# DeltaNet plus mixture of experts on one core: where the zero fills are issued, which engine scales v, and the shape of the old state's products

## Chip, cores, metric

One Trainium2 chip, one of its cores. The metric is device time in microseconds of one execution; the profile of one execution shows what its engines did. TensorE is PE (its weight loads PEld), VectorE DVE, ScalarE ACT, GpSimd POOL, SyncE SP. SP, ACT and POOL also issue DMAs; an engine executes and issues its instructions in the order in which they are written.

## The reference, cut

```python
# attention: 4 batches, 8 heads, 768 steps, head dimension 48
k_n = k / (norm(k) + 1e-6); state = 0
for t in range(S):
    y[t]  = q[t] @ state                       # output from the old state
    v_old = k_n[t] @ state
    state = state + beta[t] * outer(k_n[t], v[t] - v_old)
# then, on the 3072 rows of y (8 heads x 48 = 384 wide):
logits = x @ w_gate; e = argmax(logits); gate = softmax(logits)[e]
out = gate * (relu(x @ w1[e]) @ w2[e])         # 8 experts, 384 -> 1024 -> 384
```

## The kernel before

The 768 steps are cut into 6 blocks of 128 for each of the 4 batches: 24 tiles n = 4*tb + b. Inside a tile the recurrence is solved in four pieces of 32 steps. The main loop is a software pipeline of 27 ticks t; in tick t piece q of tile t - q is worked on, so four tiles are in flight.

The recurrence needs, for each block tb, 32 inverses of 32x32 triangular systems. `prepare(tb)` makes the scales (square roots, reciprocals) from `lg`, the products of the keys within each piece, and multiplies `lg` by row scales (line 323, 128x1024); `lanes(tb)` then does 31 column steps of multiply and subtract on DVE (lines 353 and 360) and one transpose (366) into `wt`. For block 0 `lg` comes from PE directly; for blocks 1 to 5 the products in `gg` go to DRAM `gd` (line 248) and come back as `lg` (line 251) in another layout. Each tile's `kpart` (transposes, line 217; copy to `kt`, 221; products, 259; copy to `gg`, 244) must have run first.

A tick: `residual` (PE, lines 392 and 404, and DVE line 411, which subtracts from v); `apply` (PE 419 multiplies with `wt`, ACT 423 copies to `u`); `scale_v` of the next tick (line 375, v times the norms in `nt`); `finish` of the tile three ticks back: the old state's output `yp` (line 435), the state's update (444, 448), the rest of the output (453), then the routing of its rows. `emit_slots` does the routing's small DVE steps for two tiles at a time and scatters their rows by indirect DMA (line 550, on POOL) into `xg`, a DRAM table with 448 slots for each expert, or `xt`. `xg` and `xt` are zeroed first (line 766): 7 fills of 512 rows, one of 64 and 8 of 64.

Between these, `beside(t, i)` is called seven times a tick: it runs `STEPS[i]` steps of the inverses, three steps of the routing (four from tick 20), and other pieces. The order of each engine's work is the order of the calls; nothing reorders it. Before the loop, `INIT` and `FILL` are hand-written orders of the first tiles' parts; then 56 steps of `lanes(0)`, `prepare(1)`, the rest of `lanes(0)`.

[...] After the loop the experts' products run on PE (lines 650, 660, 940); the first expert's start is fitted into the last ticks.

Of the kernel before, what the change touches and what calls it, by code (L numbers as in the profile page):

```python
# [13 lines left out]
ALU = mybir.AluOpType  # L14
# [4 lines left out]
B, H, S, D = 4, 8, 768, 48  # L19
# [21 lines left out]
def deltanet_moe(ctx, tc, q, k, v, beta, w_gate, w1, w2, out):  # L41
    nc = tc.nc
# [22 lines left out]
    zrow = cp.tile([128, ROW], F32, name="zrow")  # L65
# [41 lines left out]
    INIT = (0, 1, -2, 2, 0, 'l', 1, 'l', 'l', 3, 2, 'l', 'l', 'l', 'l', -1, 3, 'l', -1, 'l', 'l', 'l', 'l', 'l',  # L107
            -4, -1, 'l')

    STEPS = (3, 3, 2, 3, 2, 2, 2)  # L110
    W1 = 4
    DM2 = 0
    DEF = 2
# [35 lines left out]
    nt_t = lp.tile([128, (NT * B + LAG) * H], F32, name="nt_all")  # L149
# [135 lines left out]
    def prepare(tb):  # L285

        T = tiles[tb]
        if tb == 0:
            T["lg"] = fp.tile([128, 32, 32], F32, name="lg0", tag="lg", bufs=2)
        lg = T["lg"]  # L290
        lw = T["lw"]
        ss, s0, r0 = (lp.tile([128, 32], F32, name=f"{n_}{tb}", tag=n_) for n_ in ("ss", "s0", "r0"))
        if tb == 0:
            nc.vector.transpose(out=ss, in_=sst)
            yield
            nc.vector.tensor_scalar(out=ss, in0=ss, scalar1=1e-36, scalar2=None, op0=ALU.max)
        else:
            nc.vector.tensor_scalar(out=ss, in0=lg.rearrange("p a b -> p (a b)")[:, 0:1024:33],
                                    scalar1=1e-36, scalar2=None, op0=ALU.max)
        for _ in range(6 if tb > 1 else 1):  # L300
            yield
        nc.scalar.activation(out=s0, in_=ss, func=AF.Sqrt)
        yield
        nc.vector.reciprocal(r0, s0)
        yield
        nc.vector.tensor_tensor(out=r0, in0=r0, in1=ss, op=ALU.mult)
        yield
        nc.vector.tensor_tensor(out=s0, in0=s0, in1=r0, op=ALU.add)
        yield
        nc.vector.tensor_scalar(out=s0, in0=s0, scalar1=0.5, scalar2=1e-6, op0=ALU.mult, op1=ALU.add)  # L310
        yield
        nc.vector.reciprocal(r0, s0)
        yield
        nc.vector.tensor_tensor(out=ss, in0=r0, in1=bl[:, tb, :], op=ALU.mult)
        yield
        nc.vector.tensor_tensor(out=lw.rearrange("p a b -> p (a b)")[:, 0:1024:33], in0=ss, in1=r0, op=ALU.mult)
        yield
        nc.vector.tensor_tensor(out=r0, in0=ss, in1=r0, op=ALU.mult)
        yield
        if tb == 0:  # L320
            nc.vector.transpose(out=lg, in_=tiles["dg"].rearrange("p h t -> p t h"))
            yield
        nc.gpsimd.tensor_tensor(out=lg, in0=lg, in1=r0.unsqueeze(2).broadcast_to([128, 32, 32]), op=ALU.mult)  # L323
        for q in range(NB):
            p = slice(32 * q, 32 * q + 32)
            nc.vector.transpose(out=nt_t[p, (B * tb + q) * H:(B * tb + q) * H + 32], in_=s0[p])
            yield
        T["nt"] = True
# [42 lines left out]
    def scale_v(t):  # L371

        vn = vt[t]
        for r in rows(t):
            nc.gpsimd.tensor_tensor(out=vn[r], in0=vn[r], in1=nt_t[r, t * H:(t + 1) * H].unsqueeze(2)
                                    .broadcast_to([r.stop - r.start, H, D]), op=ALU.mult)

    def clear_u(n):
# [4 lines left out]
    def uview(n):  # L383
        return us[n].rearrange("t (h d) -> t h d", h=H)
# [42 lines left out]
    def finish(n):  # L427

        tb, b = n // B, n % B
        last = tb == NT - 1  # L430
        st, u = st_t[b], uview(n)
        qt, pm = qt_t[n % QSL], pm_t[n % QSL]
        yp = pss.tile([128, NP, C], F32, name=f"yp{tb}_{b}", tag="y", bufs=YB)
        for p in range(NP):
            nc.tensor.matmul(yp[:, p, :], lhsT=st[:, p, :], rhs=qt[:, p, :],  # L435
                             start=(p == 0), stop=True, skip_group_check=True)
        yield
        if not last:
            ku = pss.tile([112, NP, D], F32, name=f"ku{tb}_{b}", tag="y", bufs=YB)
            for h in range(H):  # L440

                m = 64 if h % 2 == 0 else D
                kn = tiles[tb][b]["kn"].rearrange("t h d -> t (h d)")[:, h * D:h * D + m]
                nc.tensor.matmul(ku[64 * (h % 2):64 * (h % 2) + m, h // 2, :], lhsT=kn, rhs=u[:, h, :],
                                 start=True, stop=True, skip_group_check=True)
            for a in range(2):
                r = slice(64 * a, 64 * a + D)
                nc.vector.tensor_tensor(out=st[r, :, r], in0=st[r, :, r], in1=ku[r], op=ALU.add)
            if n + NB_ < NN - B:
                load_ku(n + NB_)  # L450
        yield
        for h in range(H):
            nc.tensor.matmul(yp[64 * (h % 2):64 * (h % 2) + D, h // 2, :], lhsT=u[:, h, :], rhs=pm[:, h, :],  # L453
                             start=False, stop=True, skip_group_check=True)
        yt = lp.tile([128, NP, C], F32, name=f"yt{tb}_{b}", tag="yt", bufs=2)
        nc.scalar.copy(out=yt, in_=yp)
        yield
        w = 1 if n >= NN - W1 else 2
        if n % w == 0:
            tiles["row", n // w, w] = (rp if n < NN - 2 else xq_[0]).tile([128, 2 if n < NN - 2 else 1, ROW], F32, name=f"row{tb}_{b}", tag="row", bufs=2)  # L460
            tiles["rl", n // w, w] = lp.tile([128, 2, E], F32, name=f"rl{tb}_{b}", tag="rl", bufs=2)
        row, rl = tiles["row", n // w, w], tiles["rl", n // w, w]
        row, rl = row[:, 0:w], rl[:, 0:w]
        emit_x(n, yt, row[:, n % w], rl[:, n % w])
        if n % w == w - 1:
            fine.append(emit_slots(tb, b - w + 1, w, row, rl))
# [257 lines left out]
    NN = NT * B  # L724
# [12 lines left out]
    for i in range(NB):  # L737
        nc.sync.dma_start(out=bl[32 * i:32 * i + 32],
                            in_=beta.rearrange("b h (t i s) -> i (b h) t s", t=NT, i=NB)[i])
# [22 lines left out]
    slots = [xg[i:i + 512, :].rearrange("(g p) c -> p g c", p=128) for i in range(0, n0, 512)]  # L762
    slots.append(xg[n0:E * CAP + 512 - CAP, :].unsqueeze(1))
    slots += [xt[e * CAP + NG * 128:e * CAP + NG * 128 + 64, :].unsqueeze(1) for e in range(E)]
    for x in slots:
        nc.scalar.dma_start(out=x, in_=zrow[0:x.shape[0]].unsqueeze(1).broadcast_to(x.shape))
    while "nt" not in tiles[0]:
        run(lane)
    scale_v(0)
# [41 lines left out]
    def beside(t, i):  # L811

        inverses(STEPS[i], t)
        if before and (t, i) >= (B * before[0][0] - 5, 3):
            if not run(before[0][1], 3):
                before.pop(0)
        for _ in range(3 if t < NN - B else 4):
            if fine and not run(fine[0]):
                fine.pop(0)
        for _ in range(WSL.count((t, i))):  # L820
            run(W)
        for _ in range(ES.count((t, i))):
            ahead_step()

    fin = iter(())
    for t in range(NN + LAG):
        if t < NN and t % B == 0 and t > 0:
            while queue and queue[0][0] <= t // B:
                inverses(1, t)
            if t == NN - B:  # L830
                ep_.close()
                wq.append(ep.enter_context(tc.tile_pool(name="wr", bufs=1, side="right")))
                xq_.append(ep.enter_context(tc.tile_pool(name="xq", bufs=1, side="right")))
                W = pieces()
                run(W)
        residual(t)
        beside(t, 0)
        chunk(ks_, t)
        chunk(qs_, t)
        run(fin)  # L840
        if t + 1 < NN + LAG:
            scale_v(t + 1)
        if t + 1 < NN:
            clear_u(t + 1)
        beside(t, 1)
        copies = apply(t)
        run(copies)
        for tb in range(1, NT):
            for i in range(NB):
                if t == B * (tb - 1) + i:  # L850
                    load_v(tb, i)
        fin = finish(t - LAG) if t >= LAG else iter(())
        run(fin)
        beside(t, 2)
        run(fin)
        run(copies)
        beside(t, 3)
        chunk(ks_, t)
        beside(t, 4)
        run(fin)  # L860
        beside(t, 5)
        chunk(qs_, t)
        beside(t, 6)
    i = 0
    run(fin)
    while fine:
# [102 lines left out]
    op = ctx.enter_context(tc.tile_pool(name="op", bufs=1))  # L969
# [44 lines left out]
    for n0 in range(B * NT):  # L1014
# [3 lines left out]
                                     in_=idc, in_offset=None)  # L1018
    LP = tc.For_i(0, nblk, 1)
    LP.__enter__()  # L1020
    if True:
        ind, sel, t8 = small("ind"), small("sel"), small("t8")
        ei, j0, ce, r, rc, gi, ov = (small(n_, (128, 1)) for n_ in ("ei", "j0", "ce", "r", "rc", "gi", "ov"))
# [59 lines left out]
        for f in range(KF):  # L1083
            ps = po.tile([128, 128], F32, name="oph")
            for j in range(KD):
                nc.tensor.matmul(ps, lhsT=ow1[:, j, f * 128:(f + 1) * 128], rhs=xt[:, j, :],
                                 start=(j == 0), stop=(j == KD - 1))
            nc.scalar.activation(out=ht[:, f, :], in_=ps, func=AF.Relu)
        ps = po.tile([128, DM], F32, name="opy")
        for f in range(KF):  # L1090
# [4 lines left out]
                                     in_=yo, in_offset=None, bounds_check=N - 1, oob_is_err=False)  # L1095
# [29 lines left out]
```

## Time and profile before

| | us |
|---|---|
| median of 3 runs (604.93 to 608.1) | 607.08 |
| the profiled execution | 609.56 |
| its span, first to last instruction | 607.8 |
| busy in us: PE / DVE / ACT / POOL | 519.2 / 379.0 / 266.2 / 133.3 |

The profiled execution is 2.48 us over the median, and 1.76 us of it lie outside the span. Three stretches have to be read apart: the start up to the first line 411 at 68.1 us, the ticks up to about 355 us, and the experts after that. [...] A row "A <- B" of the waits says that A stood idle until B was done.

### The profile page before, as it was taken

The numbers are of one execution on the slowest core, as the hardware profiler recorded it, in microseconds if no ns is written. First come the engines' busy times: TensorE is split into PE (matmuls) and PEld (weight loads), VectorE is DVE, ScalarE is ACT, GpSimd is POOL, SyncE is SP. The second block draws the span as 40 slices with busy tenths as digits, with TensorE's granted clock in tenths as the row PEclk, the third lists the DMA queues.
The fourth block names the chain that finished last, engine by engine and source line by source line (L and its number), as shares of the span: only waits on it lengthen the run. The fifth ranks groups of instructions, "written<-read, shape, count | busy, mean of one in ns | idle before, by whom it ended". The sixth has DMA issues, their size and how long they took to land. (4 is left out here: it accounts for less than half of the span.)

```text
span 607.8 us, 17613 instructions
## 1 busy us (share of the span) xinstructions
PE 519.2 (85%) x7284; PEld 471.5 (78%) x7285; DVE 379.0 (62%) x1338; ACT 266.2 (44%) x506; POOL 133.3 (22%) x156
## 2 busy tenths in 40 slices
PE   7146478998988897778979989999999999999992
PEld 4035467887877786667868889999999999999992
DVE  5950898898899979994544347636272736455211
ACT  2026155664655554445643326435353625344320
POOL 2600123143333325242322111020201010101111
PEclk9559599998999988998989989999999999999996
DMA  9987348578478556448361245636373646362000
GB/s 200 309 225 129 84 103 183 109 153 207 108 156 204 121 126 147 112 92 241 118 198 56 95 145 165 191 109 200 100 204 111 189 123 184 118 172 76 23 17 24
DMA packets 153636, 85.51 MB, mean 141 GB/s; under 512 B 121565, under 2 KB 147534, under 8 KB 153552
## 3 DMA queue, kind: packets, MB, share of 16 engines
q1 hardware_dynamic: 145680, 68.22, 45.8%
q0 software_dynamic: 3456, 9.57, 4.4%
q10 hardware_dynamic: 4416, 6.56, 3.4%
q8 instruction: 58, 0.95, 0.7%
q14 instruction: 26, 0.21, 0.1%
HBM read 54.05 MB, written 24.37 MB: 129 GB/s over the span
## 5 line engine op out<-in xcount | busy, mean ns | idle before, releaser
L353 DVE TENSOR_TENSOR tmp<-lg,lw 128x84 f32<-128x84 f32 (+26 forms) x372 | 93.0, 290 | 2.0 <-POOL lg L323 1.7
L660 PE MATMUL y<-w2h,hx 128*128 128x384 f32 x352 | 93.4, 339 | 0.0
L360 DVE TENSOR_TENSOR lw<-lw,tmp 128x84 f32<-128x84 f32 (+26 forms) x372 | 85.3, 270 | 0.3
L663 POOL DMA_INDIRECT out_dram<-yo,idx x32 | 30.7, 958 | 225.7 <-ACT yo L935 170.5
L583 DVE TENSOR_TENSOR w2l<-w2r,w2h 128x768 fp32r<-128x768 f32 x32 | 31.2, 977 | 76.2 <-ACT w2h L582 76.2
L423 ACT COPY u<-ks 32x384 f32<-32x384 f32 x96 | 45.1, 470 | 46.1 <-PE ks L419 42.5
L660 PEld LDWEIGHTS y<-w2h,hx 128*128 128x128 f32 x352 | 63.9, 188 | 0.9
L650 PE MATMUL h<-xh,w1h 128*128 128x448 f32 x168 | 61.4, 365 | 0.0
L650 PE MATMUL h<-xh,w1l 128*128 128x448 f32 x168 | 61.3, 365 | 0.0
L650 PE MATMUL h<-xl,w1h 128*128 128x448 f32 x168 | 61.3, 365 | 0.0
L660 PE MATMUL y<-w2l,hx 128*128 128x384 f32 x176 | 59.0, 335 | 0.0
L419 PE MATMUL ks<-v_all,wt 32*32 32x48 f32 x1536 | 25.4, 207 | 35.6 <-DVE v_all L411 35.5
L419 PEld LDWEIGHTS ks<-v_all,wt 32*32 32x32 f32 x1536 | 21.4, 108 | 40.1 <-DVE v_all L411 38.4
L654 DVE SCALAR_TENSOR_TENSOR hx<-h,hx 128x448 fp32r<-128x448 f32 (+1 forms) x64 | 36.9, 587 | 23.7 <-ACT hx L653 23.4
L277 POOL TENSOR_SCALAR_AFFINE_SELECT pm<-pm 128x1024 f32<-128x1024 f32 x24 | 26.9, 1119 | 104.4 <-ACT pm L276 104.3
L653 ACT ACTIVATE hx<-h 128x448 fp32r<-128x448 f32 (+1 forms) x64 | 32.3, 516 | 37.2 <-PE h L650 37.2
L935 ACT ACTIVATE yo<-y,gt 128x384 f32<-128x384 f32 x22 | 12.8, 582 | 74.7 <-PE y L660 60.3
L259 PE MATMUL pg<-kt 64*128 64x128 f32 x384 | 32.4, 313 | 13.2 <-ACT kt L221 11.0
L392 PE MATMUL ks<-st,kt 128*32 128x96 f32 x768 | 43.3, 250 | 0.0
L550 POOL DMA_INDIRECT xg<-row,sli x22 | 27.5, 1251 | 63.5 <-DMA xg<-row,sli 34.0
L259 PEld LDWEIGHTS pg<-kt 64*128 64x128 f32 x384 | 27.5, 214 | 16.4 <-ACT kt L221 11.4
L392 PEld LDWEIGHTS ks<-st,kt 128*32 128x32 f32 x768 | 32.4, 110 | 3.5 <-issue 0.4
(169 smaller groups left out, 1086.2 us busy)
## 6 DMA issues: line engine op xcount, KB each, us to landing
w1r<-in_moe_w_dram SPq DMA_DIRECT2D x24, 512.0 KB, 4.1
w2r<-in_moe_w_dram SPq DMA_DIRECT2D x32, 384.0 KB, 3.4
xg<-zrow ACTq DMA_DIRECT2D x7, 788.0 KB, 7.9
kn<-in_k_dram SPq DMA_DIRECT2D x24, 192.0 KB, 5.0
qn<-in_q_dram SPq DMA_DIRECT2D x24, 192.0 KB, 4.8
xr<-xg SPq DMA_DIRECT2D x7, 591.0 KB
xn<-row SPq DMA_DIRECT2D x10, 394.0 KB
ku<-in_k_dram SPq DMA_DIRECT2D x20, 192.0 KB, 3.1
```

The source lines that it names most:

```text
L259: nc.tensor.matmul(pg[a][:, p], lhsT=kt[r, p], rhs=xt[r, p], start=True, stop=True, tile_position=(64 * a, 0), skip_group_check=True)
L353: nc.vector.tensor_tensor(out=x, in0=lg[:, r0:r1, c:c + 1].broadcast_to([128, r1 - r0, b - a]), in1=lw[:, c:c + 1, a:b].broadcast_to([128, ...
L360: nc.vector.tensor_tensor(out=lw[:, r0:r1, a:b], in0=lw[:, r0:r1, a:b], in1=x, op=ALU.subtract)
L392: nc.tensor.matmul(ks[32 * q:32 * q + 32, 2 * p:2 * p + 2, :], lhsT=kt_t[n % KSL][:, p, 32 * q:32 * q + 32], rhs=st_view(n % B, p), start= ...
L419: nc.tensor.matmul(ks[r, h, :], lhsT=tiles[n // B]["wt"][r, n % B * H + h, :], rhs=vn[r, h, :], start=True, stop=True, tile_position=(32 * ...
L423: nc.scalar.copy(out=uview(n)[r], in_=ks[r])
L583: nc.vector.tensor_tensor(out=lo, in0=src, in1=hi.bitcast(F32), op=ALU.subtract)
L650: nc.tensor.matmul(ps, lhsT=w[:, d, fs], rhs=x_[:, d], start=(n == 0), stop=(n == len(terms) - 1))
L653: nc.scalar.activation(out=hh, in_=ps, func=AF.Relu)
L654: nc.vector.scalar_tensor_tensor(out=hl, in0=ps, scalar=0.0, in1=hh.bitcast(F32), op0=ALU.max, op1=ALU.subtract)
L660: nc.tensor.matmul(ps, lhsT=h(f)[h_], rhs=w2[w][:, f, :], start=(n == 0), stop=(n == len(terms) - 1))
L663: nc.gpsimd.indirect_dma_start(out=out, out_offset=bass.IndirectOffsetOnAxis(ap=idx, axis=0), in_=yo, in_offset=None, bounds_check=N - 1, ...
```

## The change

Four edits. The 16 zero fills of `xg` and `xt` move from ACT's queue ahead of the loop to SP's queue at the end of the ticks: two after tick 0, then one a tick up to tick 14. Both multiplications on POOL, `scale_v` and the row scales of `lg`, move to DVE. The old state's output, four products of 128x128 by 128x128 whose off-diagonal 64x64 blocks are zeros, becomes eight products of 64x64 by 64x128, at the corners (0, 0) and (64, 64) of the array. And one step of the inverses moves from the fourth to the third call of `beside`, and the routing gets as many steps as the inverses there, 17 a tick and not 21, up to tick 19.

```diff
-    STEPS = (3, 3, 2, 3, 2, 2, 2)
+    STEPS = (3, 3, 3, 2, 2, 2, 2)
...
-        nc.gpsimd.tensor_tensor(out=lg, in0=lg, in1=r0.unsqueeze(2).broadcast_to([128, 32, 32]), op=ALU.mult)
+        nc.vector.tensor_tensor(out=lg, in0=lg, in1=r0.unsqueeze(2).broadcast_to([128, 32, 32]), op=ALU.mult)
...
-            nc.gpsimd.tensor_tensor(out=vn[r], in0=vn[r], in1=nt_t[r, t * H:(t + 1) * H].unsqueeze(2)
+            nc.vector.tensor_tensor(out=vn[r], in0=vn[r], in1=nt_t[r, t * H:(t + 1) * H].unsqueeze(2)
...
         for p in range(NP):
-            nc.tensor.matmul(yp[:, p, :], lhsT=st[:, p, :], rhs=qt[:, p, :],
-                             start=(p == 0), stop=True, skip_group_check=True)
+            for a in range(2):
+                r = slice(64 * a, 64 * a + 64)
+                nc.tensor.matmul(yp[r, p, :], lhsT=st[r, p, r], rhs=qt[r, p, :], start=(p == 0), stop=True,
+                                 tile_position=(64 * a, 64 * a), skip_group_check=True)
...
-    for x in slots:
-        nc.scalar.dma_start(out=x, in_=zrow[0:x.shape[0]].unsqueeze(1).broadcast_to(x.shape))
...
-        for _ in range(3 if t < NN - B else 4):
+        for _ in range(STEPS[i] if t < NN - B else 4):
             if fine and not run(fine[0]):
                 fine.pop(0)
...
         chunk(qs_, t)
         beside(t, 6)
+        for x in slots[t + 1 if t else 0:t + 2]:
+            nc.sync.dma_start(out=x, in_=zrow[0:x.shape[0]].unsqueeze(1).broadcast_to(x.shape))
```

ACT's order at the start, before: behind the copy of tile 3's `kt` stand the 16 fills, then the copies of tiles 4 and 5 and of their products.

```order
L302 ACTIVATE s_250<-ss_249 128x32
L221 COPY kt_125<-pt_3_291 128x512
L766 DMA xg<-zrow 128x4x394 x7
L766 DMA xg<-zrow 64x394
L766 DMA xt<-zrow 64x394 x8
L221 COPY kt_126<-pt_0_445 128x512
L221 COPY kt_127<-pt_1_452 128x512
L244 COPY gg_104<-pg_0_0_459 128x4x128
```

The same place now:

```order
L302 ACTIVATE s_250<-ss_249 128x32
L221 COPY kt_125<-pt_3_291 128x512
L221 COPY kt_126<-pt_0_429 128x512
L221 COPY kt_127<-pt_1_436 128x512
L244 COPY gg_104<-pg_0_0_443 128x4x128
```

The fills are gone from between them; nothing else of ACT's order there differs.

DVE's order where block 0's scales end and its column steps begin, before and now. `r_251` holds the row scales, `s_250` the norms, `nt_all` their transpose.

```order
L318 TENSOR_TENSOR r_251<-ss_249,r_251 128x32
L321 STREAM_TRANSPOSE lg_248<-dg 128x1024
L326 STREAM_TRANSPOSE nt_all<-s_250 32x32 x4
L353 TENSOR_TENSOR tmp_0_594<-lg_248,lw_183 128x15
L353 TENSOR_TENSOR tmp_0_594<-lg_248,lw_183 128x16
```

```order
L318 TENSOR_TENSOR r_251<-ss_249,r_251 128x32
L321 STREAM_TRANSPOSE lg_248<-dg 128x1024
L323 TENSOR_TENSOR lg_248<-lg_248,r_251 128x1024
L326 STREAM_TRANSPOSE nt_all<-s_250 32x32 x4
L375 TENSOR_TENSOR v_all<-v_all,nt_all 32x384
L353 TENSOR_TENSOR tmp_0_578<-lg_248,lw_183 128x15
```

Both multiplications now stand on DVE ahead of the column steps; line 375 reads the first load of v.

SP's order around the end of tick 0, now (line 866 is the fills' new place; before, the same rows stood there without it):

```order
L177 DMA qn_120<-in_q_dram 128x8x48
L381 DMA u_784<-zrow 96x384
L201 DMA v_all<-in_v_dram 32x32x48
L866 DMA xg<-zrow 128x4x394 x2
L174 DMA kn_118<-in_k_dram 128x8x48
L177 DMA qn_121<-in_q_dram 128x8x48
L381 DMA u_898<-zrow 96x384
L201 DMA v_all<-in_v_dram 32x24x48
L203 DMA v_all<-in_v_dram 32x8x48
L866 DMA xg<-zrow 128x4x394
```

The loads of the next tick's keys, queries and v stand behind the fills.

## The prediction

> **What bounds the kernel now.** I read the busy time by stretches first (columns: PE, PEld, DVE, ACT and POOL busy, then the granted clock, the share of the DMA engines and GB/s).
>
> ```profile
> 0.00:20.00 20.00, 11.27 (x285) 6.82 (x286) 12.25 (x42) 3.95 (x7) 6.34 (x21) 0.95 0.97 228
> 20.00:40.00 20.00, 3.02 (x14) 2.22 (x16) 18.38 (x104) 1.07 (x2) 6.64 (x17) 0.50 0.95 267
> 40.00:60.00 20.00, 16.22 (x169) 13.36 (x166) 0.19 (x1) 11.32 (x22) 0.82 (x1) 0.86 0.89 160
> 100.00:120.00 20.00, 18.96 (x476) 17.04 (x476) 17.74 (x78) 12.61 (x27) 5.70 (x5) 1.00 0.70 153
> 400.00:500.00 100.00, 100.00 (x540) 94.31 (x539) 47.74 (x76) 42.61 (x70) 12.04 (x13) 1.00 0.50 149
> ```
>
> From 400 us on PE never stops, and no edit touches that. In the ticks DVE and PE are both near full. The start is odd: from 20 to 40 DVE works and PE and ACT stand, from 40 to 60 it is the other way round. Then the waits:
>
> ```profile
> PE ks L419 <- DVE v_all L411: 35.5, 16, 10.2
> ACT kt L221 <- DMA esel<-in_moe_w_gate_dram: 27.8, 1, 27.8
> DVE ss L298 <- DMA lg<-gd: 25.4, 5, 21.4
> ```
>
> and the start in order of time:
>
> ```profile
> 9.80 12.60 SPq L174 DMA_DIRECT2D kn<-in_k_dram  x4
> ...
> 11.01 20.50 ACTq L766 DMA_DIRECT2D xg<-zrow  x7
> 11.36 0.19 DVE L306 TENSOR_TENSOR r<-r,ss 128x32 f32<-128x32 f32 x1
> ...
> 18.88 0.27 DVE L353 TENSOR_TENSOR tmp<-lg,lw 128x15 f32<-128x15 f32 x2 [1.27 <-POOL lg L323]
> ...
> 21.83 1.11 PE L217 MATMUL pt<-ident,kn 128*128 128x128 f32 x4 [6.82 <-DMA kn<-in_k_dram]
> ...
> 38.04 0.34 DVE L360 TENSOR_TENSOR lw<-lw,tmp 128x48 f32<-128x48 f32 x2
> 38.57 1.07 ACT L221 COPY kt<-pt 128x512 f32<-128x512 f32 x2 [27.80 <-DMA esel<-in_moe_w_gate_dram]
> ...
> 40.64 0.82 POOL L375 TENSOR_TENSOR v_all<-v_all,nt_all 32x384 f32<-32x384 f32 x1 [13.53 <-DMA v_all<-in_v_dram]
> ...
> 50.88 2.60 SPq L248 DMA_DIRECT2D gd<-gg  x4
> ```
>
> ```profile
> 59.74 0.19 DVE L298 TENSOR_SCALAR ss<-lg 128x32 f32<-128x32 f32 x1 [21.36 <-DMA lg<-gd]
> ...
> 63.12 2.05 DVE L353 TENSOR_TENSOR tmp<-lg,lw 128x36 f32<-128x36 f32 x2
> ...
> 68.11 0.52 DVE L411 TENSOR_TENSOR v_all<-v_all,ks 32x384 f32<-32x384 f32 x1
> ...
> 71.56 0.41 DVE L353 TENSOR_TENSOR tmp<-lg,lw 128x84 f32<-128x84 f32 x2
> ...
> 72.20 0.42 DVE L353 TENSOR_TENSOR tmp<-lg,lw 128x96 f32<-128x96 f32 x2
> ```
>
> This is the whole case. Tile 4's keys, asked for from 9.80, reach PE at 21.83, since the fills fill the DMA engines (share 0.97). ACT's instruction stream sits in issuing fills until 38.57 (the row's name is the last counter it waited on), though tile 4's transposes lay ready at 22.9. Only then do `kt`, the products, `gd` (50.88) and `lg` (59.74) follow, and DVE, done with its 56 steps at 38.38, stands for 21.36 us. The first tick's line 411 comes at 68.11.
>
> In the ticks DVE is stretched. Its instructions take longer while POOL computes:
>
> ```profile
> 101.72 1.09 POOL L277 TENSOR_SCALAR_AFFINE_SELECT pm<-pm 128x1024 f32<-128x1024 f32 x1 [8.02 <-ACT pm L276]
> 101.73 1.12 DVE L306 TENSOR_TENSOR r<-r,ss 128x32 f32<-128x32 f32 x1
> ...
> 113.16 1.05 DVE L353 TENSOR_TENSOR tmp<-lg,lw 128x96 f32<-128x96 f32 x2
> ...
> 113.24 0.85 POOL L375 TENSOR_TENSOR v_all<-v_all,nt_all 128x384 f32<-128x384 f32 x1
> ```
>
> ```profile
> 133.10 2.52 DVE L353 TENSOR_TENSOR tmp<-lg,lw 128x84 f32<-128x84 f32 x2
> ...
> 133.45 1.11 POOL L277 TENSOR_SCALAR_AFFINE_SELECT pm<-pm 128x1024 f32<-128x1024 f32 x1
> 134.12 0.75 PEld L419 LDWEIGHTS ks<-v_all,wt 32*32 32x32 f32 x64
> 134.12 0.88 PE L419 MATMUL ks<-v_all,wt 32*32 32x48 f32 x64
> ...
> 134.51 0.84 POOL L375 TENSOR_TENSOR v_all<-v_all,nt_all 128x384 f32<-128x384 f32 x1
> 134.93 0.97 PEld L435 LDWEIGHTS yp<-qt,st 128*128 128x128 f32 x8
> 134.93 1.16 PE L435 MATMUL yp<-qt,st 128*128 128x128 f32 x8
> ...
> 136.62 1.16 PE L259 MATMUL pg<-kt 64*128 64x128 f32 x16
> ```
>
> Line 306 takes 0.19 us alone and 1.12 beside the select; the pair of 128x96 takes 0.42 alone and 1.05 beside `scale_v`; the pair of 128x84 takes 0.41 alone and 2.52 where select and `scale_v` come in a row. So POOL's work costs DVE nearly its own length: 0.93 a select, 0.63 to 0.84 a `scale_v`.
>
> **The change part by part. Fills off ACT, the start.** Durations for the sum:
>
> ```profile
> L411 DVE TENSOR_TENSOR v_all<-v_all,ks 128x384 f32<-128x384 f32 (+3 forms) x28 | 15.4, 551 | 10.5 <-issue 4.0 <-POOL pm L277 4.0 <-PE ks L404 2.2
> L323 POOL TENSOR_TENSOR lg<-lg,r 128x1024 f32<-128x1024 f32 x6 | 11.5, 1911 | 44.3 <-DVE r L318 31.5 <-DVE nt_all L326 12.8
> L583 DVE TENSOR_TENSOR w1l<-w1r,w1h 128x1024 fp32r<-128x1024 f32 x24 | 29.5, 1229 | 7.5 <-ACT w1h L582 7.0
> ```
>
> ```profile
> q10 hardware_dynamic: 4416, 6.56, 3.4%
> ...
> kn<-in_k_dram SPq DMA_DIRECT2D x24, 192.0 KB, 5.0
> ```
>
> ```profile
> 279.91 0.55 DVE L411 TENSOR_TENSOR v_all<-v_all,ks 128x384 f32<-128x384 f32 x1 [0.79 <-PE ks L404]
> ```
>
> A load of keys lands 5.0 us after its issue in the median, so tile 4's, issued at 9.80, comes at about 15 (15.5 with the 1 MB of `lw` zeros ahead of it). At the 160 GB/s of 40 to 60, where loads of this kind ran alone, 192 KB take 1.2 us: tile 7's keys come at 19 and the first load of v, four loads behind tile 4's, at 20.5 to 21. That load matters now, because line 375 stands on DVE ahead of block 0's column steps: DVE would be there at about 18.9, as before (line 323 takes 1.2 there by line 583's row, where POOL took 1.9 beside DVE's short transposes), waits until 21, and multiplies for 0.5; behind it stand block 0's column steps, and behind those the whole first tick. SP asks for v after `esel`, whose zeros and copies stood on POOL behind line 323, till 18.88, and now run at the very start; so v is not late for that. The 56 steps take 38.38 - 18.88 = 19.5 us, so DVE is through at 41.0.
>
> When is `lg` there? From ACT's release at 38.57 to the first `gd` were 12.3 us of PE and ACT. That chain now starts when tile 4 is transposed, 16.6, and reaches `gd` at 28.9. SP has 2.06 MB of v and keys ahead of it, from 20 on at 160 GB/s, to 32.9. From `gd`'s issue to line 298 were 8.86 us. So `lg` is there between 37.8 and 41.8, near DVE's 41.0; I take no wait. From line 298 to line 411 were 8.37 us, less 1.7 for the stretched pair (2.05, and 0.33 by its neighbours), plus 1.2 for line 323 on DVE: 7.9. First line 411 at 48.9 and not 68.11: **-19.2 us**. Best end: v in time and `lg` too, 46.8, -21.3. Worst: PE's chain half again as long, 18.5, since the clock was 0.50 from 20 to 40, and `gd` 2 us late behind keys: `lg` at 46, line 411 at 53.9, -14.
>
> **Both multiplications on DVE, the ticks.** Ticks 0 to 20 run from 68.11 to 279.91 with DVE the fuller engine. Added: 20 `scale_v` at 0.55 (line 411, same shape) = 11.0, and 4 of line 323 at 1.2 = 4.9; 15.9. Taken away: 20 stretches of 0.63 to 0.84 where a `scale_v` meets a DVE instruction, say 17 of them at 0.7 = 11.9, and 4 of line 323's, worth 1.7 - 0.6 = 1.1 at 63.12, = 4.4; 16.3. **Net -0.4, call it 0**; ends -8.5 (every one at its full 0.84 and 1.91) and +6 (half of them meet nothing). The select stays on POOL and still costs 0.9.
>
> **Fills in the ticks.** The old queue moved 6.56 MB in 3.4% of 607.8, 20.7 us of all 16 engines, so one fill of 788 KB takes 2.5 us of a 10 us tick whose share is 0.70: 0.95 for seven ticks. Behind it on SP stand the next tick's loads, each needed one to four ticks later, but `gd` and `lg` of blocks 2 and 3 have only about a tick: their line 298 waited 4.0 us over four blocks (25.4 less 21.4) already. The first scatter, in tick 6, waits on POOL for the last of the seven fills, with a select behind it whose result line 453 reads three ticks later. Fill 7 is ordered after that scatter and holds SP once until it lands; behind it stand keys and queries with a tick or more to spare. **+1**, ends 0 and +6.
>
> **Old state's output.** Eight records in 1.16 us now; sixteen of half the rows and half the columns after. At line 259 sixteen records with 64 rows, in pairs, take the same 1.16; at line 419, 64 records at four diagonal places take 0.88. So pairs run side by side: **-0.5** over 24 tiles; ends -3 (weights half as wide) and the rival below.
>
> **Steps.** No instruction more or less. A pair of tiles needs 32 routing steps and gets 34 in two ticks, not 42; the routing's DVE work spreads over both ticks of a pair. PE's waits for line 411 at line 419, 25 us without the first, are what that can shorten: **-0.5**, ends -5 and +1. The two scatters of a pair move apart; from tick 20 nothing differs.
>
> Sum: -19.2 + 0 + 1 - 0.5 - 0.5 = -19.2 on the profiled 609.56, which is 590.4. The runs' median is 2.5 lower; against it, 607.1 - 19.2 = **588**.
>
> **Rivals.** *Serial corners* (other side). If the two corners of a pair don't overlap, sixteen records take twice 1.16 less one record's tail, 2.0 us, +0.87 a tile, and 21 tiles on a nearly full PE give back 18 us; with DVE's upper end (+6), about 612. It decides if the pairs of line 435 start 100 ns apart, not together. [...] Line 419's four row strips also write one bank and overlap in the trace, so I give it 4 in 100; line 259, whose halves write two banks, would not settle it.
> *DVE pays in full.* If POOL's stretch is not what `scale_v` frees, because the select or a scatter takes its place, 15.9 come back: 603. For it: selects and scatters stay. Against: 113.16, where `scale_v` stood alone. 7 in 100.
> *The stall only shrinks.* `lg` at 50, since `gd`'s 128 KB pieces queue behind v and keys: half the 21 us stay, 598. 10 in 100.
> *More is won*: ticks shorten with the evener routing, and each `scale_v` frees its full length: 576. 12 in 100.
>
> **Numbers.** Forecast 67 in 100 (583 to 594). Range 577 to 600. Half a per cent is 3 us, about what a measurement of this kernel can tell from none: slower with serial corners (4), same with DVE paying in full and `lg` late (3), faster 93.
>
> **What would show it.** Right: no fills on ACT; line 298's first wait under 3 us; first line 411 at 47 to 51; no stretched pair over 1.6 us like that of 133.10; ticks 0 to 20 within 6 us of 212; line 435's successor 1.0 to 1.2 us a tile. Wrong: DVE waiting long for v ahead of line 375; waits for `lg` of blocks 2 and 3 over 4 us each; pairs 100 ns apart.

## The result, and the profile after

| | before | after |
|---|---|---|
| median, one chip | 606.0 us (4 runs, 604.43 to 608.1) | 584.98 us (4 runs, 582.3 to 587.85) |
| on a second chip | 606.62 (17 runs) | 585.86 (6 runs) |
| ratio, with 95% interval | | 0.9652 [0.9586, 0.9717]; second chip 0.9683 [0.9637, 0.973] |
| span of the profiled execution | 607.8 | 581.4 |
| first line 411 / ticks 0 to 20 / ticks 21 to 27 / rest | 68.1 / 211.8 / 56.1 / 271.8 | 48.4 / 210.4 / 50.4 / 272.1 |

The change takes 3.2 to 3.5% off, some 21 us; forecast were 588 us, 577 to 600. In this table and the ones below, "ticks 0 to 20" runs from the first line 411 to that of tick 21, and "ticks 21 to 27" from there to the last tick's line 411 (counted from 0, the last tick is 26).

The busy time by stretches (PE, PEld, DVE, ACT, POOL; granted clock, DMA share, GB/s):

```profile
0.00:20.00 20.00, 14.47 (x310) 8.70 (x311) 12.27 (x34) 5.12 (x9) 8.08 (x36) 0.88 0.90 170
20.00:40.00 20.00, 14.10 (x158) 11.73 (x156) 18.91 (x109) 11.21 (x21) 0.00 (x0) 0.93 0.98 158
40.00:60.00 20.00, 10.77 (x92) 9.68 (x94) 15.09 (x76) 4.39 (x9) 1.09 (x1) 0.51 0.47 132
100.00:120.00 20.00, 19.32 (x540) 17.05 (x528) 19.24 (x90) 12.83 (x27) 4.62 (x3) 1.00 0.84 190
```

The two halves of the old start, DVE alone and then PE and ACT alone, now lie on top of each other: from 20 to 40 all three work. In order of time:

```profile
16.25 1.23 DVE L323 TENSOR_TENSOR lg<-lg,r 128x1024 f32<-128x1024 f32 x1
16.77 0.59 ACT L221 COPY kt<-pt 128x512 f32<-128x512 f32 x1 [6.28 <-PE pt L217]
17.48 2.85 SPq L201 DMA_DIRECT2D v_all<-in_v_dram  x4
21.09 0.55 DVE L375 TENSOR_TENSOR v_all<-v_all,nt_all 32x384 f32<-32x384 f32 x1 [2.83 <-DMA v_all<-in_v_dram]
28.77 3.07 SPq L248 DMA_DIRECT2D gd<-gg  x4
34.46 0.34 SPq L251 DMA_DIRECT2D lg<-gd  x1
40.53 0.18 DVE L298 TENSOR_SCALAR ss<-lg 128x32 f32<-128x32 f32 x1
48.41 0.52 DVE L411 TENSOR_TENSOR v_all<-v_all,ks 32x384 f32<-32x384 f32 x1
```

ACT copies tile 4 at 16.77 and not at 38.57, `gd` is issued at 28.77 and not at 50.88, and line 298 follows DVE's column steps with no wait. The only wait left at the start is 2.83 us for v. The waits and the groups of the whole run:

```profile
PE ks L419 <- DVE v_all L411: 34.0, 16, 12.6
DVE v_all L411 <- PE ks L404: 10.4, 6, 4.3
DVE ss L298 <- DMA lg<-gd: 7.6, 4, 2.4
```

```profile
L353 DVE TENSOR_TENSOR tmp<-lg,lw 128x84 f32<-128x84 f32 (+26 forms) x372 | 82.0, 261 | 0.3
L360 DVE TENSOR_TENSOR lw<-lw,tmp 128x84 f32<-128x84 f32 (+26 forms) x372 | 78.6, 252 | 0.3
```

and of the kernel before:

```profile
L353 DVE TENSOR_TENSOR tmp<-lg,lw 128x84 f32<-128x84 f32 (+26 forms) x372 | 93.0, 290 | 2.0 <-POOL lg L323 1.7
L360 DVE TENSOR_TENSOR lw<-lw,tmp 128x84 f32<-128x84 f32 (+26 forms) x372 | 85.3, 270 | 0.3
```

The same 744 column steps take 160.6 us instead of 178.3, so 17.7 us of them had been stretching. The two multiplications now add 24.4 to DVE (17.0 of line 375 and 6 times 1.23 of line 323), and other DVE instructions got shorter too, so that DVE's busy time for the whole run hardly moves: 379.0 before, 376.6 after. In ticks 3 and 4 of the changed kernel:

```profile
76.27 1.09 PE L438 MATMUL yp<-qt,st 64*64 64x128 f32 x16
...
87.86 1.50 PE L419 MATMUL ks<-v_all,wt 32*32 32x48 f32 x64 [3.16 <-DVE v_all L411]
89.29 1.97 PE L438 MATMUL yp<-qt,st 64*64 64x128 f32 x16
```

Sixteen records of the old state's output take 1.09 us at a granted clock of 1.00 (76.2 to 77.4). Behind the 3.16 us in which PE stood idle PE's instructions take 1.6 to 1.8 times as long for some 5 us, at a granted clock of 0.50 (87.8 to 93.0): line 419 1.50 us, line 438 1.97, line 447 1.09 and line 259 1.92, where from 99.7 to 103.3 they take 0.88, 1.09, 0.67 and 1.16.

### The profile page after: what moved, and what is told of

Same layout as the page of the kernel before. It is cut to its first block, busy times and chain, and to the rows that moved or that the text cites. A ratio compares the mean times of both kernels' runs of the same rounds, so it can differ in the third digit from the quotient of the medians.

```text
span 581.4 us, 17976 instructions
## 1 busy us (share of the span) xinstructions
PE 517.5 (89%) x7476; PEld 467.5 (80%) x7477; DVE 376.6 (65%) x1372; ACT 266.1 (46%) x506; POOL 97.4 (17%) x122
## 4 chain that ended last, share of the span: by engine, by line
PE 54%; DVE 23%; DMA 11%; issue 4%; SPq 3%; ACT 2%; POOL 0%; POOLq 0%; DVEq 0%; ACTq 0%
PE h L653 19%; PE y L663 16%; DVE tmp L353 6%; DVE lw L360 6%; PE y L943 4%; DMA gd<-gg 3%; DMA lg<-gd 3%; PE ks L419 2%; PE yp L438 2%; DMA xg<-row,sli 2%; DVE wt L366 2%; SPq L248 2%; PE ks L392 2%; DMA xr<-xg 1%; PE pg L259 1%
## 5 line engine op out<-in xcount | busy, mean ns | idle before, releaser
L353 DVE TENSOR_TENSOR tmp<-lg,lw 128x84 f32<-128x84 f32 (+26 forms) x372 | 82.0, 261 | 0.3
L360 DVE TENSOR_TENSOR lw<-lw,tmp 128x84 f32<-128x84 f32 (+26 forms) x372 | 78.6, 252 | 0.3
L419 PE MATMUL ks<-v_all,wt 32*32 32x48 f32 x1536 | 27.7, 215 | 34.3 <-DVE v_all L411 34.0
L277 POOL TENSOR_SCALAR_AFFINE_SELECT pm<-pm 128x1024 f32<-128x1024 f32 x24 | 32.5, 1356 | 149.4 <-ACT pm L276 149.4
L419 PEld LDWEIGHTS ks<-v_all,wt 32*32 32x32 f32 x1536 | 23.4, 114 | 39.2 <-DVE v_all L411 37.6
L938 ACT ACTIVATE yo<-y,gt 128x384 f32<-128x384 f32 x22 | 12.8, 582 | 73.3 <-PE y L663 59.1
L553 POOL DMA_INDIRECT xg<-row,sli x22 | 23.4, 1064 | 93.4 <-DVE sli L546 55.7
L244 ACT COPY gg<-pg 128x512 f32<-128x512 f32 x48 | 25.7, 588 | 19.7 <-PE pg L259 19.5
L586 DVE TENSOR_TENSOR w1l<-w1r,w1h 128x1024 fp32r<-128x1024 f32 x24 | 29.5, 1229 | 7.7 <-ACT w1h L585 7.2
```

Source lines behind the costliest of these rows:

```text
L277: nc.gpsimd.affine_select(out=pm, in_=pm, compare_op=ALU.is_gt, fill=0.0, base=0, pattern=[[0, H], [1, C]], channel_multiplier=-1)
L353: nc.vector.tensor_tensor(out=x, in0=lg[:, r0:r1, c:c + 1].broadcast_to([128, r1 - r0, b - a]), in1=lw[:, c:c + 1, a:b].broadcast_to([128, ...
L360: nc.vector.tensor_tensor(out=lw[:, r0:r1, a:b], in0=lw[:, r0:r1, a:b], in1=x, op=ALU.subtract)
L419: nc.tensor.matmul(ks[r, h, :], lhsT=tiles[n // B]["wt"][r, n % B * H + h, :], rhs=vn[r, h, :], start=True, stop=True, tile_position=(32 * ...
L586: nc.vector.tensor_tensor(out=lo, in0=src, in1=hi.bitcast(F32), op=ALU.subtract)
```

## The experiments: each edit alone

Four kernels, each the kernel before with one of the four edits, on one chip (before there: 604.56, 25 runs).

**Fills alone** (`e1_fills`): line 766's loop out, line 866's in.

> The kernel before with one edit: the zero fills go from ACT ahead of the loop to SP at the ticks' ends; both multiplications stay on POOL. My theory: the start's stall is made by the fills alone. ACT copies tile 4's kt at 17, but esel's zeros still stand on POOL behind line 323 (18.9), so v and all of SP's loads behind it start at 22; gd is issued at about 33 to 34, lg lands at 42 to 43, and DVE, whose column steps wait for nothing and end at 38.4, idles 4 to 5 us. First line 411 at 51 to 52, not 68.1; the ticks about as before plus 1; total about 606 - 16 = 590. Rival, that the fills in the ticks cost as much as they free: 600 or more. Rival, that the multiplications' move was needed for the start: first line 411 at 58 or later.

**Both multiplications on DVE alone** (`e2_dve`): `nc.gpsimd` to `nc.vector` at lines 323 and 375.

> The kernel before with one edit: lines 323 and 375 on DVE, the fills still on ACT at the start. My theory: DVE stands at line 375 until v lands at 40.6, so block 0's 56 steps run from 41.2 to 60.7 and lg (59.7) is there by then; first line 411 at 68.6, the stall has only changed its name. In the ticks DVE's stretched instructions shrink by about 16 us and 15.9 us of work come in: ticks 0 to 20 within 6 us of 212. Total 606 within 4. Rival, POOL's stretch isn't freed: ticks 0 to 20 some 228, total 622. Rival, more is won than I counted: ticks 0 to 20 about 203, total 597.

**Corners alone** (`e3_corners`): lines 435 to 439 of the changed kernel.

> The kernel before with one edit: the old state's output as eight 64x64 products at two corners. My theory: pairs run side by side, sixteen records in 1.1 us against eight in 1.16; ticks about 0.07 us shorter where PE bounds them; total 606 less 0 to 2, which can't be told from none. Rival, serial corners in one bank: sixteen records in 2.0 us and 620 or more.

**Steps alone** (`e4_steps`): `STEPS = (3, 3, 3, 2, 2, 2, 2)` and `range(STEPS[i] ...)`.

> The kernel before with one edit: the routing's steps 17 a tick and not 21, and one step of the inverses moved from the fourth to the third call. My theory: even ticks go from 8.2 to about 9.3 us and odd ones from about 13 to 11.5, the sum of a pair loses 0 to 0.5 us since DVE is full in both; total 606 less 0 to 5. Rival, the last ticks gain from scatters that come one at a time: ticks 21 to 27 shorter than 56.1 by 3 or more. Rival, later scatters make the end later: total 608 or more.

| | us | ratio to before | first line 411 | ticks 0 to 20 |
|---|---|---|---|---|
| fills | 591.35 | 0.9793 [0.9732, 0.9853] | 49.7 | 214.3 |
| DVE | 609.21 | 1.0085 [1.0053, 1.0118] | 73.2 | 208.7 |
| corners | 603.69 | 1.0001 [0.9964, 1.0038] | 64.4 | 213.2 |
| steps | 602.07 | 0.9952 [0.9913, 0.999] | 64.6 | 211.2 |

The fills alone are worth 12.5 us. With them gone from ACT, the start looks as in the changed kernel, with 1.94 us of waiting left where 4 to 5 were expected:

```profile
31.30 3.96 SPq L248 DMA_DIRECT2D gd<-gg  x4
41.34 0.19 DVE L298 TENSOR_SCALAR ss<-lg 128x32 f32<-128x32 f32 x1 [1.94 <-DMA lg<-gd]
```

The corners are worth nothing that can be measured. The DVE edit alone costs 5 us, all of it at the start; in the ticks it gains 3. Its start:

```profile
24.37 9.59 SPq L201 DMA_DIRECT2D v_all<-in_v_dram  x4
...
33.79 0.55 DVE L375 TENSOR_TENSOR v_all<-v_all,nt_all 32x384 f32<-32x384 f32 x1 [15.60 <-DMA v_all<-in_v_dram]
...
44.69 1.07 ACT L221 COPY kt<-pt 128x512 f32<-128x512 f32 x2 [33.71 <-issue]
...
56.52 2.60 SPq L248 DMA_DIRECT2D gd<-gg  x4
...
65.27 0.19 DVE L298 TENSOR_SCALAR ss<-lg 128x32 f32<-128x32 f32 x1 [11.96 <-DMA lg<-gd]
```

Line 375 on DVE waits 15.6 us for v behind the fills, and the column steps behind it. I missed something here: ACT also came free 6 us later (44.69, not 38.57). `esel`, whose zeros no longer stand behind POOL's work, was asked for sooner, so SP's loads of v and keys went among the fills instead of behind them, and the last fills were issued at 44.66. So this edit needs the first one: what it gains in the ticks it loses at the start as long as the fills are there.

The product of the four ratios is 0.983, the whole change has 0.965 to 0.968. About 10 us come from the edits together. Some 8 of them are likely the DVE edit's loss at the start (5 us slower in all with 3 won in the ticks), which vanishes with the fills; the last group of runs adds what the steps are worth beside the other edits.

## The experiments: what held the start

The prediction named two things that the old fills did: they filled the DMA engines, and they held ACT's instruction stream. To tell them apart, and to price the wait for v, three kernels ran beside the changed one.

**The changed kernel again** (`after_again`): no edit.

> The changed kernel once more, so that the three others can be set against it on one chip. Both theories: 585 us, within 0.5%; first line 411 at 48 to 49, ticks 0 to 20 about 210.

**Late v** (`e7_late_v`):

```diff
-    scale_v(0)
     clear_u(0)
...
     run(lane, 56)
+    scale_v(0)
```

> The changed kernel, but the first scaling of v stands on DVE behind the 56 column steps of block 0 and not ahead of them. Theory (DVE is the longer of the two chains to line 298, and the 2.83 us that it waits for v at line 375 lie on it): DVE reaches line 298 at 38.2 instead of 40.5, the first line 411 comes at 46.2, and the time falls by 2.3 us to about 583. Rival (lg lands no sooner than DVE now asks for it): line 298 waits about 2 us for lg where it waited for nothing, the first line 411 stays at 48.4, and the time is the same within 1 us.

**Fills at the old place, from POOL** (`e6_pool_start`): late v, and

```diff
+    for x in slots:
+        nc.gpsimd.dma_start(out=x, in_=zrow[0:x.shape[0]].unsqueeze(1).broadcast_to(x.shape))
     while "nt" not in tiles[0]:
...
-        for x in slots[t + 1 if t else 0:t + 2]:
-            nc.sync.dma_start(out=x, in_=zrow[0:x.shape[0]].unsqueeze(1).broadcast_to(x.shape))
```

> As the kernel with the late scaling of v, but all 16 fills are issued at their old place ahead of the loop, from POOL's queue, which has nothing else to do there; none is left in the ticks. It separates the two things that the old fills did at the start: they filled the DMA engines, and they held ACT's instruction stream. Theory (ACT's stream was what cost): tile 4's keys come late, near 22 as before, so the chain to gd is about 6 us later, gd issued at 34 to 36, lg there at 43 to 45, the first line 411 at 51 to 54; with the ticks 2 to 4 us shorter without fills, 584 to 590 in all. Rival (the full DMA engines alone did it): gd no sooner than 48, line 298 waits 15 us or more, the first line 411 at 62 or later, 598 or more.

| | us | ratio to before (606.62) | first line 411 | ticks 0 to 20 |
|---|---|---|---|---|
| changed kernel | 585.86 | 0.9683 [0.9637, 0.973] | 48.4 | 210.4 |
| late v | 584.42 | 0.9655 [0.9611, 0.9699] | 46.7 | 210.0 |
| late v, fills from POOL | 600.4 | 0.9902 [0.9865, 0.9938] | 64.3 | 207.0 |

Late v moves the first line 411 by 1.7 us (2.2 were expected), and line 298 still waits for nothing, so `lg` was there before 38.8:

```profile
38.80 0.17 DVE L298 TENSOR_SCALAR ss<-lg 128x32 f32<-128x32 f32 x1
```

The time falls by 1.4 us, which the intervals don't separate from nothing.

My theory of the fills fell. Nothing is queued behind them on POOL, ACT is free throughout, and yet the old start is back (POOL issues the fills at line 769 of this kernel):

```profile
9.41 6.02 POOL L769 DMA_DIRECT2D xg<-zrow  x8
...
29.57 1.12 PE L217 MATMUL pt<-ident,kn 128*128 128x128 f32 x4 [14.19 <-DMA kn<-in_k_dram]
...
30.73 0.58 ACT L221 COPY kt<-pt 128x512 f32<-128x512 f32 x1 [20.22 <-PE pt L217]
...
35.58 1.12 PE L217 MATMUL pt<-ident,kn 128*128 128x128 f32 x4 [4.89 <-DMA kn<-in_k_dram]
...
47.70 2.81 SPq L248 DMA_DIRECT2D gd<-gg  x4
...
56.46 0.19 DVE L298 TENSOR_SCALAR ss<-lg 128x32 f32<-128x32 f32 x1 [16.66 <-DMA lg<-gd]
```

POOL had issued its first eight fills by 15.4. SP asked for tile 4's keys at 9.88, when only the first of them had been started, and still these keys reached PE at 29.57 and not at 21.83; tile 5's followed at 35.58. From 16 to 28 us the DMA engines were full, and nearly all that they moved were fills: 4.06 MB of POOL's queue (q0) and 0.24 MB of SP's (q1):

```profile
q0 software_dynamic: 968, 4.06, 94.5%
q1 hardware_dynamic: 1276, 0.24, 11.0%
```

So the fills' 6.56 MB are enough to bring the old start back even when another engine asks for them. What ACT's held stream added in the kernel before, this run doesn't tell, since it isn't the old start with ACT set free: there the 16 fills were issued more slowly, up to 38.5, and the keys came sooner. Tile 4's stood transposed at 22.9 and tile 5's at 28.3, and both then waited for ACT until 38.57:

```profile
27.13 1.12 PE L217 MATMUL pt<-ident,kn 128*128 128x128 f32 x4 [4.19 <-DMA kn<-in_k_dram]
...
31.54 6.99 ACTq L766 DMA_DIRECT2D xt<-zrow  x8
```

Over the runs the first line 411 stands at 64.3 us with the fills in POOL's queue, at 64.4 to 68.1 with them in ACT's, and at 46.7 with them gone from the start (late v in the first and the last).

## The experiments: the fills in the ticks

**Large fills in a gap** (`e11_fills_gap`): from 34.9 to 48.6 us SP issues nothing in the changed kernel. The eight `xg` fills go there, ahead of `run(lane, 56)`:

```diff
+    for x in slots[0:8]:
+        nc.sync.dma_start(out=x, in_=zrow[0:x.shape[0]].unsqueeze(1).broadcast_to(x.shape))
     lane = lanes(0)
     run(lane, 56)
...
-        for x in slots[t + 1 if t else 0:t + 2]:
+        for x in slots[max(8, t + 1):t + 2]:
```

> The changed kernel, but the eight fills of xg are issued from SP ahead of the 56 column steps, where SP issues nothing from 35 to 48.6 us; the eight small ones of xt stay at the ends of ticks 7 to 14. Theory (the large fills in ticks 0 to 6 hold back gd and lg of blocks 2 and 3 and with them PE, which then runs at a lower clock for some us): line 298's waits of blocks 2 and 3 fall from 2.4 and 2.2 to the 0.6 and 1.3 of the kernel before, PE is not at half its rate around 88 to 93, ticks 0 to 20 take 206 to 208 instead of 210.4, and the time is about 582. Rival (those waits and the low clock come from DVE's order in ticks 3 and 4, not from the fills, or the fills now hold the loads of ticks 0 and 1): ticks 0 to 20 within 1.5 of 210.4 and the time the same within 1.5 us.

**All fills there, and late v** (`e12_all_gap_late_v`): `for x in slots:` there, none in the ticks, and the edit of late v. This was put together as the version that might beat the changed kernel.

> A version put together from the runs so far: the first scaling of v stands behind the 56 column steps, and all 16 fills are issued from SP ahead of those steps, where SP issues nothing from 35 to 48.6 us; none is left in the ticks. Theory (the fills of the ticks cost what the two kernels without them, 207.0 and 208.7 us for ticks 0 to 20, suggest): first line 411 at 46.7, ticks 0 to 20 at 207, 581 in all, 0.7% under the changed kernel. Rival (nothing hangs on the fills in the ticks; the loads of ticks 0 and 1 now stand behind 6.4 MB): first line 411 at 46.7, ticks 0 to 20 at 210 or more, 584 or more.

| | us | ratio to before | first line 411 | ticks 0 to 20 |
|---|---|---|---|---|
| large fills in the gap | 584.95 | 0.9653 [0.9606, 0.97] | 48.8 | 209.0 |
| all in the gap, late v | 586.75 | 0.9659 [0.9613, 0.9705] | 46.5 | 213.0 |

The second ran on the chip of the next section, where the kernel before takes 605.8.

The rival was right both times. With the large fills gone from the ticks, line 298 waits no less than with them (7.6 and, in the changed kernel again, 5.5):

```profile
DVE ss L298 <- DMA lg<-gd: 7.7, 4, 3.0
```

So nothing shows that the fills make those waits. Nor is it shown that the order does: they differ between two executions of the changed kernel. For blocks 2 and 3 they were 2.4 and 2.2 us in the first profile and 0.4 and 1.0 in the second, in which PE didn't run at half its rate in tick 4 either (its page has the clock at 9 tenths from 87.4 to 102.0, the first profile's at 7). And with all 16 in the gap the loads of ticks 0 and 1 stand behind them. SP issues the small fills until 58.6, and PE waits for the zeros of tile 2's `u`:

```profile
46.88 11.70 SPq L779 DMA_DIRECT2D xt<-zrow  x8
...
61.58 0.87 SPq L381 DMA_DIRECT2D u<-zrow  x1
...
65.12 0.61 PE L404 MATMUL ks<-u,gg 128*32 128x48 f32 x10 [4.03 <-DMA u<-zrow]
```

Tick 1 takes 11.4 us instead of 8.6. Neither version can be told from the changed kernel. The kernel with no fills in the ticks and none in their loads' way (from POOL, above) has 207.0 against 210.0 of late v. By that pair the fills cost some 3 us in the ticks, but it is one profile of each, and the kernel with all 16 in the gap doesn't bear it out: without the 2.8 us lost in tick 1 its ticks come to 210.2, with no fill in them. So the price lies between nothing and 3 us.

## The experiments: three edits undone

Each is the changed kernel with one edit taken back, on a third chip (before: 605.8, 11 runs).

**v scaled on POOL** (`e8_scale_pool`): line 375 back to `nc.gpsimd`.

> The changed kernel with the scaling of v (line 375) back on POOL; the scaling of lg (line 323) stays on DVE. Theory (a stretched DVE instruction costs more than the 0.55 us of the scaling itself): the first line 411 at 46.7, since line 375 no longer stands on DVE ahead of the column steps; ticks 0 to 20 at 213 to 214 instead of 210.4; DVE's excess over its undisturbed durations, 12.3 us, back at 25 or more; 587 to 588 in all, 0.3% over the changed kernel. Rival (the two prices cancel, as forecast): ticks 0 to 20 at 210 to 211 and 584 in all.

**lg scaled on POOL** (`e13_lg_pool`): line 323 back to `nc.gpsimd`.

> The changed kernel with the scaling of lg (line 323) back on POOL, the scaling of v stays on DVE. Theory: four of them lie in the ticks; each takes POOL 1.9 us and stretches what DVE does beside it by 1 to 1.7, and DVE then waits for its end where the column steps come next; block 1's lies in the start, first line 411 at 49.5 to 50.5, ticks 0 to 20 at 211 to 214, 587 to 589 in all. Rival (it is hidden beside the transposes): 48.4, 210 and 585.

**Old steps** (`e10_old_steps`): `STEPS = (3, 3, 2, 3, 2, 2, 2)` and `range(3 if t < NN - B else 4)`.

> The changed kernel with the old table of steps and three routing steps at each call. Theory (the evener routing is worth what it was worth alone, 2.9 us): odd ticks back over 12 us and even ones under 9, ticks 0 to 20 at 213, 588 to 589 in all. Rival (with DVE less stretched the long odd ticks have room): ticks 0 to 20 within 1 us of 210.4, 585 to 586.

| | us | ratio to before | first line 411 | ticks 0 to 20 |
|---|---|---|---|---|
| v on POOL | 588.63 | 0.97 [0.9654, 0.9746] | 47.4 | 219.2 |
| lg on POOL | 588.54 | 0.9703 [0.967, 0.9735] | 50.5 | 212.2 |
| old steps | 591.78 | 0.9773 [0.9737, 0.9809] | 48.5 | 212.1 |

The excess of DVE that the first expectation speaks of is a sum over its instructions in ticks 0 to 20: what each took beyond the lower quartile of the same line and shape. Counted so from the traces it is 32.8 us before, 11.4 after, 26.2 with v on POOL and 15.3 with lg on POOL; the expectation has 12.3 for the 11.4. The groups say the same (v on POOL):

```profile
L353 DVE TENSOR_TENSOR tmp<-lg,lw 128x84 f32<-128x84 f32 (+26 forms) x372 | 90.0, 282 | 0.4
L360 DVE TENSOR_TENSOR lw<-lw,tmp 128x84 f32<-128x84 f32 (+26 forms) x372 | 83.7, 265 | 0.3
```

So 13.1 us of the column steps' 17.7 are line 375's. The scaling itself is 17.0 us of DVE's time in the whole run. The two nearly cancel in DVE's busy time, and still this kernel is slower by 9 us in the profiled ticks (of an execution 3.6 us over its median), by 0.2 to 0.5% in the medians. A scaling on POOL also stands in POOL's queue, with line 411 on DVE behind it:

```profile
DVE v_all L411 <- issue: 6.2, 4, 2.5
DVE v_all L411 <- PE ks L404: 5.1, 3, 3.0
DVE v_all L411 <- POOL pm L277: 4.0, 1, 4.0
```

These are 15.3 us of idle DVE ahead of line 411, where the changed kernel has 10.4 in one profile and 13.3 in the other. The medians' intervals overlap those of the changed kernel, so a loss is likely and not shown. Likewise lg on POOL, of which 2.1 us lie in the start.

The steps are the surprise. Undone, they cost 0.9 to 1.2%, 5.5 to 7 us, and this interval lies clear of the changed kernel's on both other chips, 0.9652 [0.9586, 0.9717] and 0.9683 [0.9637, 0.973]. Alone on the old kernel they gave 0.5%. The odd ticks are long again: ticks 7, 9 and 11 take 12.2, 12.2 and 12.8, the even ones between them 8.5 to 8.8, but their sum is only 1.6 us more in this profile, whose execution (586.0) was the fastest of its six. Where the rest of the median's loss lies was not seen.

## What scatters in ticks 21 to 27

Ticks 21 to 27 took 56.1 us before and 50.4 after, though only the corners and line 375 differ there. One wait decides most of it: in tick 23 PE transposes the rows that the first expert reads back from `xg`. In the kernel before, in the changed one, and in the one with all fills in the gap:

```profile
PE xt L674 <- DMA xr<-xg: 3.2, 1, 3.2
```

```profile
282.22 0.41 PE L677 MATMUL xt<-ident,xr 128*128 128x128 f32 x2 [1.17 <-DMA xr<-xg]
```

```profile
284.67 0.66 PE L677 MATMUL xt<-ident,xr 128*128 128x128 f32 x2 [3.55 <-DMA xr<-xg]
...
285.87 1.95 PE L456 MATMUL yp<-pm,u 128*48 128x128 f32 x16
```

In the profiles of this case in which that wait stays at 1.0 to 1.3 us, tick 23 takes 10.0 to 10.4; where it reaches 2.7 or more, 12.0 to 14.8, mostly with PE slow for some us afterwards (line 456 above takes 1.95 us, and 1.08 in tick 3 of the changed kernel). One lies between, 1.9 and 11.7. Both kinds occur with the old and the new order, late v (2.73) among them. So 3.7 us of the difference between the two profiled spans, tick 23's 13.9 and 10.2, should not be put down to the change. For the same reason the 3 us that the steps alone gain there (52.9 for 56.1, a rival that its expectation named) are not the steps': the corners alone, with the old steps, have 50.6. That an earlier load would hold the short form was not tried.

## Why the prediction was right, and where not

- **The start, -19.2.** Right in mechanism and place: `gd` at 28.8 (forecast 28.9), v's wait to 21.1 (21), no wait at line 298, first line 411 at 48.4 (48.9). The old start it was taken from was long, though: in the profiles of the two kernels that leave the start as it was (corners, steps) the first line 411 stands at 64.4 and 64.6. The gain is 16 to 19.7. The sum took the gain of an execution 2.5 us over the median off the median itself; that step was wrong by up to 3 us. Its account of the old start is shown in part: the full DMA engines alone are enough to bring it back (e6); what ACT's held stream added stays open.
- **Both multiplications on DVE, 0.** In ticks 0 to 20 the multiplications added 16.4 us to DVE (15.9 forecast) and its other instructions got shorter by 22.7 (16.3 forecast), 15.2 of these in the column steps: DVE's busy time there fell from 190.9 to 184.6. So the mechanism was right and what it frees was put too low. The longest pair in the ticks fell from 2.80 to 1.42, and the selects still stretch DVE: the pair of 1.42, at 190.41 beside the select of 190.40, takes 0.49 alone (63.53). (The end of +6 was worked too low as well: with half of 16.3 gone, +7.7.) The net in the time, by e8 and e13, is likely a gain of 2 to 6 us, not shown and inside the ends, since a shorter wait counts and not only a shorter busy time; the wait for v moves the first line 411 by 1.7 (e7).
- **Fills in the ticks, +1.** Between nothing and 3, inside its ends. The waits for `lg` of blocks 2 and 3 that it named grew in one profile of the changed kernel and not in the other, and taking the large fills out of the ticks (e11) didn't shorten them.
- **Old state's output, -0.5.** No effect, 1.0001. The pairs run side by side at 1.09 us (the two products of a pair start 7 ns apart in the trace, not 100), so the serial rival fell: no run shows its 2.0 us.
- **Steps, -0.5.** The mis-sized term: -2.9 alone, -5.5 to -7 in the changed kernel, by medians of different chips. The furthest end named was -5, so there the term lies outside its ends. Ticks 0 to 20 of the profile show only 1.6 of it; the cause of the rest stays open.

The forecast of 588 came within 3 us of 584.98 with errors of opposite sign, so part of its closeness is luck: the start was taken up to 3 us too large, the steps 2 to 6 us too small and the multiplications likely 2 to 6 us too small.

## What to carry to other kernels

Large transfers that nobody needs yet should not stand beside the loads that the first work waits for; here, asking for them from another engine's queue left the start as late as it was (first line 411 at 64.3 us, against 64.4 to 68.1). Where two engines stretch each other's instructions, as POOL's work did DVE's column steps here (178.3 us before, 160.6 after), sum the busy time of the victim's unchanged instructions on both sides before deciding where an operation goes, and price the start separately, since an operation that is neutral in the loop can wait for a load there (line 375 2.83 us for v, and 15.60 with the fills in front). When a start or a wait differs between executions, take the gain from the usual one.

## What the hardware showed that was not expected

PE's half rate behind a wait: after 3.16 us of idle PE, line 438's sixteen records took 1.97 us instead of 1.09, and the granted clock was 0.50 from 87.8 to 93.0 (0.83 over 80 to 100). So a wait of 3 us can cost more than itself. A wait of 2.43 us in the same profile was followed by the same (231.2 to 233.6; the granted clock is 0.50 from 233.8 to 237.2), and not every such wait is: after 2.57 us in the kernel before, line 419's 64 records took 0.88 us (at 254.55), and the granted clock was 1.00 from 252 to 258. And the select on POOL, untouched by the change, takes longer now, 1356 ns in the mean against 1119 before:

```profile
L277 POOL TENSOR_SCALAR_AFFINE_SELECT pm<-pm 128x1024 f32<-128x1024 f32 x24 | 32.5, 1356 | 149.4 <-ACT pm L276 149.4
```

It was the other way round before: all 24 selects took 1.09 to 1.28 us, and one beside a column step made DVE the slower (the pair of line 360 at 121.56 takes 1.38 us beside the select of 121.61, and 0.49 alone at 82.44). Now 19 of the 24 selects take 1.08 to 1.19 us, and five take 1.7 to 2.6. These five all start while column steps follow one another on DVE without a gap; the one at 200.28, of 2.58 us, lasts over ten of them. That POOL waits there for DVE is my estimate from these start times, and was not tested; here the longer selects are hidden behind POOL's 149 us of idle time.
